# A fused attention and gated feed-forward kernel on one core: value means moved from TensorE to VectorE and DRAM, the sums' check moved up, the order planned anew

## The chip, the cores and the metric

The kernel runs on one core of a Trainium2 chip. The core has four engines that compute (TensorE, VectorE, ScalarE and GpSimd, in the rows PE, DVE, ACT and POOL), a fifth, SyncE (SP), that issues most of the transfers, and 16 DMA engines that carry them out. PE has two rows: PE for matmuls and PEld for the weight loads that go with them. The metric is the time of one execution on the device in microseconds. The kernel before has a median of 662.69 us over three runs (660.53, 662.69 and 663.2).

## The reference

There are four batch elements, eight heads, 768 rows of sequence and 64 columns per head. Attention is a local window of 15 rows to each side joined with 24 summaries of blocks of 32 rows: the key of a summary is the elementwise maximum over its block, its value the mean. The rows of the output, 3072 tokens of 512, then go through a feed-forward of width 2048 whose activation is h - tanh(h).

```python
k_sum = k.reshape(B, H, nb, 32, D).max(axis=3)
v_sum = v.reshape(B, H, nb, 32, D).mean(axis=3)
scores_l = q @ k.T / 8, masked to |i - j| < 16
scores_s = q @ k_sum.T / 8 + log(32)
a = softmax(concat(scores_l, scores_s)); x = a @ concat(v, v_sum)
h = x @ w_in; out = (h - tanh(h)) @ w_out
```

## The kernel before

The sequence is cut into eight units `u` of 384 rows, two for each of the four batch elements `b = u // 2`. A unit has four pairs of heads `p`, and two groups `g` of four heads each. For each pair there is a chain: queries and keys are turned (by TensorE for u = 0 and 1, by VectorE after that), the block maxima are taken (`top max`), scores are formed on TensorE (`scores`), VectorE takes row minima (`min`), ScalarE exponentials (`exp`), the rows are normalized (`normal`), the probabilities turned (`p turn`: TensorE for u = 0 and 1, and VectorE with a trip through DRAM after that), and `values` multiplies them with the tile `vw`, which holds the window's rows of v and, in its first 24 partitions, the 24 means. `x split` writes the result as a high and a low float32r part.

The feed-forward runs 22 slots behind. For each unit there are 16 columns `f` of 128: `in` forms h in the tile pH by 12 matmuls of 384 columns, ScalarE and VectorE or GpSimd make the activation of it, it is split into a high and a low part (`gh`, `gl`), and `out` adds the product with w_out into three tiles pY by 9 matmuls of 512 columns (for u = 0 by three full float32 ones, which the trace shows as two records each). While u = 0 and 1 run, the 32 weight tiles are loaded and converted from float64 by VectorE, ScalarE and GpSimd (`w scale`, `w low`, `w sign`, `w join`, `w high part`, `w low part`).

**The value means.** For b = 0 and 1, `first_means` loads v of a group as one transfer, adds pairs of rows (`pair`, on GpSimd), and `sum_means` adds the rest up with three float32 matmuls against a 0 and 1/32 matrix that lies in the buffer `vacc` (task `sum`); ScalarE copies the result to `mean`. For b = 2 and 3, `sum_chunks` loads a group in four chunks into `tmp`, and VectorE adds eight rows at a time into `vacc` (task `chunk sum`); then `finish_v` turns the sums by four matmuls against the identity (task `mean turn`), and ScalarE scales them by 1/32 into `mean`. `put_mean` carries `mean` into `vw`: two copies for u = 0, one DMA (`mean put`) from then on.

**The sums' check.** The activation is a series that holds for small h. ScalarE collects the sum of h squared of every `in`. At the end VectorE takes the maximum over all of them (`seen`), TensorE turns it (`seen turn`), VectorE takes the maximum again (`seen max`), and every engine loads that number into a register and branches: if it is too large, the whole work is done again in a more general form. The last three copies of pY and their stores stand behind this load in program order, and the branch behind them.

**The order.** Tasks are recorded with their costs and dependencies; `Plan.schedule` then lays them out on five engines by a list schedule, taking the ready task of the highest level. A level is the longest path to the end by the tasks' costs, plus a number per task from the table `BIAS` and one per kind and phase from `KB`. While TensorE would be idle in the first 100 us, the planner puts in matmuls on the identity (`keep_warm`, in the order `pX<-ident`). Each engine then runs its list strictly in order, with semaphores between the lists. All instructions are issued through one helper, which is why every row of the profile has line 65.

Of the kernel before, what the change touches and what calls it, by code (L numbers as in the profile page):

```python
# [10 lines left out]
F32 = mybir.dt.float32  # L11
# [10 lines left out]
SLOTS = 4  # L22
# [295 lines left out]
def program(  # L318
# [211 lines left out]
    def convert(i):  # L530
# [41 lines left out]
        def join():  # L572
            low, _, w = words()
            vector.scalar_tensor_tensor(at(to[0]).bitcast(U32), w.bitcast(U32), 3, low, op0=ALU.logical_shift_left, op1=ALU.bitwise_or)
        either("w scale", {ACT: 0.59, DVE: 0.335, POOL: 1.25}, scale, r=[RAW[1]], w=[(tmp, 0)])
        do("w low", DVE, 0.335, low_bits, w=[RAW[0]])
        either("w sign", {DVE: 0.57, ACT: 1.15}, sign, r=[RAW[1]], w=[RAW[0]])
        do("w join", DVE, 0.66, join, r=[RAW[0], (tmp, 0)], w=[to])
        if not whole:
            either("w high part", {ACT: 0.52, DVE: 0.335, POOL: 1.25}, lambda e: copy(e, at(res)[:, 0], at(tmp)), r=[(tmp, 0)], w=[(res, 0)])  # L580
            either("w low part", {POOL: 1.225, DVE: 0.602}, lambda e: e.tensor_tensor(at(res)[:, 1], at(tmp), at(res)[:, 0].bitcast(F32), op=ALU.subtract), r=[(tmp, 0), (res, 0)], w=[(res, 1)])
# [57 lines left out]
    def first_means(b, g):  # L639
        base = ("V", b, g)  # L640
        buf(base, "vsum1", [P, HG, 6 * D]) if b else buf(base, "xh", [P, HG, 6 * D], F32, 2)
        dma("v load", lambda e: e.dma_start(at(base), v[b, HG * g:HG * (g + 1)].rearrange("h (r t) d -> r h (t d)", t=6)), S * HG * D * 4, 1536, w=[(base, 0)])

        def pairs():
            x = at(base).rearrange("p h (t two d) -> p (h t) two d", two=2, d=D)
            return x[:, :, 0], x[:, :, 1]
        either("pair", {POOL: 1.77, DVE: 0.87}, lambda e: e.tensor_tensor(pairs()[0], *pairs(), op=ALU.add), w=[(base, 0)])

    def sum_means(b, g, tag):
        base, ps = ("V", b, g), bank(("mv", b, g), tag)  # L650
# [7 lines left out]
        do("mean out", ACT, 0.39, lambda: scalar.activation(mean[32 * g:32 * g + NB], at(ps)[:NB, :HG * D], AF.Copy), r=[(ps, 0)], w=[MEAN[g]])  # L658


    def sum_chunks(b, g):
        acc = buf(("acc", b, g), "vacc", [P, 2, D])
        for c in range(4):
# [489 lines left out]
```

## Time and profile before

| | |
|---|---|
| median of three runs | 662.69 us |
| the profiled execution's own time | 662.02 us |
| its span | 660.3 us |
| mean granted TensorE clock | 0.995 |
| PE, PEld busy | 98%, 83% |
| DVE, ACT, POOL busy | 50%, 59%, 28% |
| HBM read, written | 54.39 MB, 15.73 MB |

The rows are of one execution, whose own time is 662.02 us; 1.7 us of it lie outside the span of its instructions. A busy share is an average over a start in which transfers and the small chains of the first unit set the pace, a stretch in which the weights are converted beside the feed-forward of the first unit, and a long even stretch. A matmul record's end is modelled and consecutive records overlap, so what a matmul costs in a dense stretch is the distance from its start to the next start, which the chain of waits shows for runs of records.

### The profile page before, as it was taken

The numbers are of one execution on the slowest core, as the hardware profiler recorded it, in microseconds if no ns is written. First come the engines' busy times: TensorE is split into PE (matmuls) and PEld (weight loads), VectorE is DVE, ScalarE is ACT, GpSimd is POOL, SyncE is SP. The second block draws the span as 40 slices with busy tenths as digits, with TensorE's granted clock in tenths as the row PEclk, the third lists the DMA queues.
The fourth block names the chain that finished last, engine by engine and source line by source line (L and its number), as shares of the span: only waits on it lengthen the run. The fifth ranks groups of instructions, "written<-read, shape, count | busy, mean of one in ns | idle before, by whom it ended". The sixth has DMA issues, their size and how long they took to land.

```text
span 660.3 us, 14416 instructions
## 1 busy us (share of the span) xinstructions
PE 646.4 (98%) x5301; PEld 550.2 (83%) x5301; DVE 331.1 (50%) x1070; ACT 390.1 (59%) x1166; POOL 186.9 (28%) x190
## 2 busy tenths in 40 slices
PE   8999999999999999999999999999999999999995
PEld 6676666688888888889888888898989899899994
DVE  4898898998745675435454543314332433111111
ACT  4898889766546656465555636455654736364442
POOL 3030313134334232233223133322322313122221
PEclk9899999999999999999999999999999999999999
DMA  9978876653665665253453631423303331000001
GB/s 283 242 222 239 221 209 200 100 126 97 143 132 111 158 140 133 62 157 93 84 118 73 171 78 38 93 84 90 78 13 93 108 92 49 1 32 17 1 1 51
DMA packets 157163, 73.18 MB, mean 111 GB/s; under 512 B 120768, under 2 KB 147360, under 8 KB 157088
## 3 DMA queue, kind: packets, MB, share of 16 engines
q1 hardware_dynamic: 156816, 72.01, 43.7%
q8 instruction: 43, 0.70, 0.5%
q14 instruction: 32, 0.26, 0.1%
q10 hardware_dynamic: 272, 0.20, 0.1%
HBM read 54.39 MB, written 15.73 MB: 106 GB/s over the span
## 4 chain that ended last, share of the span: by engine, by line
PE 87%; DMA 5%; DVE 3%; ACT 2%; SPq 1%; issue 1%; POOL 0%; ACTq 0%; DVEq 0%
PE pY L65 39%; PE pH L65 39%; PE pS L65 3%; PE pT L65 3%; PE pX L65 2%; DMA xl<-in_k_dram 2%; DMA raw<-in_moe_w_out_dram 1%; SPq L65 1%; DMA tmp<-in_v_dram 1%; DMA raw<-in_moe_w_in_dram 1%; ACT tmp L65 1%; ACT raw L65 1%; DVE prob L65 1%; DVE tmp L65 0%; DVE raw L65 0%
## 5 line engine op out<-in xcount | busy, mean ns | idle before, releaser
L65 PE MATMUL pH<-xh,w 128*128 128x384 f32 x1024 | 269.6, 344 | 0.4 <-POOL w L65 0.4
L65 PEld LDWEIGHTS pH<-xh,w 128*128 128x128 f32 x1024 | 184.9, 188 | 15.1 <-issue 3.1
L65 POOL TENSOR_TENSOR gl<-gu,gh 128x384 fp32r<-128x384 f32 x112 | 114.2, 1020 | 253.0 <-ACT gh L65 232.7
L65 PE MATMUL pY<-wf,gh 128*128 128x512 f32 x411 | 168.5, 441 | 0.0
L65 DVE TENSOR_TENSOR gu<-gu,gt 128x384 f32<-128x384 f32 x72 | 40.9, 568 | 218.7 <-ACT gu L65 199.8
L65 PE MATMUL pH<-xl,w 128*128 128x384 f32 x448 | 150.6, 336 | 0.0
L65 ACT ACTIVATE gu<-pH 128x384 f32<-128x384 f32 x128 | 62.6, 489 | 146.5 <-PE pH L65 138.4
L65 ACT ACTIVATE gh<-gu 128x384 fp32r<-128x384 f32 x109 | 57.2, 525 | 72.6 <-DVE gu L65 40.1
L65 PEld LDWEIGHTS pY<-wf,gh 128*128 128x128 f32 x411 | 76.6, 188 | 24.9 <-issue 14.1
L65 ACT ACTIVATE prob<-prob,stats 128x118 f32<-128x118 f32 x207 | 78.2, 385 | 14.2 <-DVE stats L65 14.1
L65 PEld LDWEIGHTS pH<-xl,w 128*128 128x128 f32 x448 | 84.0, 188 | 0.0
L65 POOL TENSOR_TENSOR gu<-gu,gt 128x384 f32<-128x384 f32 x40 | 41.3, 1031 | 119.0 <-ACT gu L65 113.6
L65 ACT ACTIVATE gu<-gu 128x384 f32<-128x384 f32 x128 | 67.0, 523 | 0.0
L65 ACT ACTIVATE gt<-pH 128x384 f32<-128x384 f32 x128 | 62.0, 484 | 0.8 <-PE pH L65 0.8
L65 PE MATMUL pY<-kT,gh 128*128 128x512 f32 x126 | 50.4, 400 | 0.0
L65 PE MATMUL pY<-kT,gl 128*128 128x512 f32 x126 | 49.6, 394 | 0.3 <-POOL gl L65 0.3
L65 DVE TENSOR_SCALAR prob<-prob,stats 128x118 f32<-128x118 f32 x177 | 49.3, 344 | 0.8
L65 PE MATMUL pY<-vsum,gh 128*128 128x512 f32 x105 | 41.8, 398 | 0.0
L65 PE MATMUL pY<-vsum,gl 128*128 128x512 f32 x105 | 40.9, 390 | 0.0
L65 ACT ACTIVATION_READ_ACCUMULATOR prob<-prob,stats 128x1 f32 x192 | 36.5, 190 | 0.0
L65 DVE CUSTOM_DVE_ANT_0 prob<-pS,mask 128x118 f32<-128x118 f32 x96 | 25.4, 277 | 17.5 <-PE pT L65 16.2
L65 DVE TENSOR_SCALAR raw<-raw 128x512 uint32<-128x512 uint32 (+1 forms) x51 | 28.4, 570 | 2.2 <-DMA raw<-in_moe_w_out_dram 1.0
(155 smaller groups left out, 961.3 us busy)
## 6 DMA issues: line engine op xcount, KB each, us to landing
place<-turned SPq DMA_DIRECT2D x96, 96.0 KB, 1.9
probT<-place SPq DMA_DIRECT2D x24, 384.0 KB, 3.5
raw<-in_moe_w_in_dram SPq DMA_DIRECT2D x16, 512.0 KB, 4.0
raw<-in_moe_w_out_dram SPq DMA_DIRECT2D x16, 512.0 KB, 4.5
vw<-in_v_dram SPq DMA_DIRECT2D x80, 96.0 KB, 4.2
out_dram<-tmp SPq DMA_DIRECT2D x23, 256.0 KB, 2.1
rawq<-in_q_dram SPq DMA_DIRECT2D x96, 48.0 KB, 2.1
raw<-in_k_dram SPq DMA_DIRECT2D x48, 96.0 KB, 2.9
```

The source lines that it names most:

```text
L65: return lambda *args, **kwargs: self._tc.keep_in_program_order(op(*args, **kwargs))
```

## The change

For b = 1 to 3, all value means now come from `sum_chunks`: VectorE adds eight rows of a chunk into the second half of `vacc`, and a second instruction scales by 1/32 and adds to the first half (or, for the first chunk, only scales). The sums leave `vacc` by a DMA to DRAM (`mean save`, 96 rows of 256 bytes, written in the order of blocks), and `mean put` reads them from there for u = 2 to 7. `finish_v` is gone, and `first_means` and `sum_means` are called for b = 0 alone. The chunks of b = 1 are recorded while u = 1 is scored.

The three tasks of the check are recorded ahead of the last `out` (function `look`), and the `out` tasks of the second and third tile wait until `seen turn` has been issued. The last copies and stores still follow the load.

The planner's costs of a dozen kinds are changed, and `BIAS`, `SL` and `KB` are new tables.

```diff
-BIAS = {('const', 0): -83.15, ('const', 1): 88.23, ('const', 2): -15.03, ...
+BIAS = {('const', 0): 151, ('const', 1): 13.25, ('const', 2): 155, ...
...
-        either("w sign", {DVE: 0.57, ACT: 1.15}, sign, r=[RAW[1]], w=[RAW[0]])
-        do("w join", DVE, 0.66, join, r=[RAW[0], (tmp, 0)], w=[to])
+        either("w sign", {DVE: 0.54, ACT: 1.1}, sign, r=[RAW[1]], w=[RAW[0]])
+        do("w join", DVE, 0.61, join, r=[RAW[0], (tmp, 0)], w=[to])
...
-        buf(base, "vsum1", [P, HG, 6 * D]) if b else buf(base, "xh", [P, HG, 6 * D], F32, 2)
+        buf(base, "xh", [P, HG, 6 * D], F32, 2)
...
     def sum_chunks(b, g):
         acc = buf(("acc", b, g), "vacc", [P, 2, D])
...
-                vector.tensor_reduce(m[:, 1 if c else 0], x.rearrange("r t d -> r d t"), axis=AX.X, op=ALU.add)
+                vector.tensor_reduce(m[:, 1], x.rearrange("r t d -> r d t"), axis=AX.X, op=ALU.add)
                 if c:
-                    vector.tensor_tensor(m[:, 0], m[:, 0], m[:, 1], op=ALU.add)
-            do("chunk sum", DVE, 1.22 if c else 0.97, total, w=[(st, 0), (acc, 0)])
-
-    def finish_v(b, g):
-        acc, ps = ("acc", b, g), bank(("mv", b, g), "pT")
-
-        def go():
-            for hh in range(HG):
-                tensor.matmul(at(ps)[:NB, D * hh:D * (hh + 1)], ident[:96, NB * hh:NB * (hh + 1)], at(acc)[:96, 0], start=True, stop=True)
-        do("mean turn", PE, 0.557, go, r=[(acc, 0), IDENT], w=[(ps, 0)])
-        do("mean out", ACT, 0.39, lambda: scalar.activation(mean[32 * g:32 * g + NB], at(ps)[:NB, :HG * D], AF.Copy, scale=1.0 / 32), r=[(ps, 0)], w=[MEAN[g]])
+                    vector.scalar_tensor_tensor(m[:, 0], m[:, 1], 1.0 / 32, m[:, 0], op0=ALU.mult, op1=ALU.add)
+                else:
+                    vector.tensor_scalar(m[:, 0], m[:, 1], 1.0 / 32, None, op0=ALU.mult)
+            do("chunk sum", DVE, 1.25 if c else 1.1, total, w=[(st, 0), (acc, 0)])
+        place = buf(("means", b, g), "means", [NB, HG, D], F32, 2 * NG, scratch)
+        dma("mean save", lambda e: e.dma_start(at(place).rearrange("n h d -> h n d"), at(acc)[:96, 0]), 96 * 256, 256, r=[(acc, 0)], w=[(place, 0)])
...
+        if u >= WHOLE:
+            place = ("means", u // 2, g)
+            dma("mean put", lambda e: e.dma_start(at(vw)[:NB].rearrange("r i f h d -> r (i f) (h d)"), at(place).rearrange("n h d -> n (h d)").unsqueeze(1).broadcast_to([NB, 2 * NT, HG * D])), 2 * NT * NB * HG * D * 4, 1024, r=[(place, 0)], w=[vw_keys(vw, i, half)[2] for i in range(NT) for half in range(2)])
+            return
...
-            do("out", PE, 0.86 if whole else 0.702, go, r=keys, w=[(y, 0)])
+            do("out", PE, 0.86 if whole else 0.702, go, r=keys, w=[(y, 0)], before=[t for t in plan.tasks if t.kind == "seen turn" and i])
...
+    def look():
+        st, ps = share(("st", "seen"), "stats", 2, lambda n: made[("stats",)][:, n]), bank(("seen",), "pT")
+        do("seen", DVE, 0.2, lambda: vector.tensor_reduce(at(st)[:, 0:1], sums_seen, axis=AX.X, op=ALU.max), r=[(SEEN, n) for n in range(NM)], w=[(st, 0)])
+        do("seen turn", PE, 0.1, lambda: tensor.transpose(at(ps)[:1, :P], at(st)[:, 0:1], ident), r=[(st, 0), IDENT], w=[(ps, 0)])
+        do("seen max", DVE, 0.2, lambda: vector.tensor_reduce(seen, at(ps)[:1, :P], axis=AX.X, op=ALU.max), r=[(ps, 0)])
...
+            if small_only and m2 == (NU - 1, NF - 1):
+                look()
             moe_out(*m2)
...
-        if B > 1 and j in (20, 28):
-            first_means(1, (j - 20) // 8)
-            sum_means(1, (j - 20) // 8, "pT")
-        if s0 is not None and not early and s0[0] % 2 == 1 and 1 < s0[0] < NU - 1:
+        if s0 is not None and not early and s0[0] % 2 == 1 and s0[0] < NU - 1:
             b, (n, c) = s0[0] // 2 + 1, divmod(j % (NP * SLOTS), SLOTS)
             if n % 2 == 0 and c == 0:
                 sum_chunks(b, n // 2)
-            elif n % 2 == 1 and c == SLOTS - 1:
-                finish_v(b, n // 2)
-
-    if small_only:
-
-        st, ps = share(("st", "seen"), "stats", 2, lambda n: made[("stats",)][:, n]), bank(("seen",), "pT")
...
```

At the start, SP's queue, before: `xl<-in_k_dram` is the keys of one pair of heads of u = 0 (the row with x2 is those of the second and third pair), `xh<-in_v_dram` a whole group of v for the means of b = 0, `vw` the window's rows of v, `raw` a weight tile.

```order
L65 DMA rawq_108<-in_q_dram 128x2x192
L65 DMA xl<-in_k_dram 128x2x384
L65 DMA vw_128<-in_v_dram 16x4x64
L65 DMA rawq_96<-in_q_dram 128x2x192
L65 DMA xl<-in_k_dram 128x2x384 x2
L65 DMA xh<-in_v_dram 128x4x384 x2
L65 DMA raw<-in_moe_w_in_dram 128x4x256
L65 DMA xl<-in_k_dram 128x2x384
L65 DMA vw_98<-in_v_dram 16x4x64
L65 DMA vw_98<-in_v_dram 96x4x64 x2
```

All four pairs' keys stand ahead of the window's rows of v, the last behind one weight tile. The same stretch of SP's queue now, from the keys of the second pair on (those of the first pair and 192 KB of queries stand ahead of it):

```order
L65 DMA xl<-in_k_dram 128x2x384
L65 DMA rawq_130<-in_q_dram 128x2x192
L65 DMA xh<-in_v_dram 128x4x384 x2
L65 DMA raw<-in_moe_w_in_dram 128x4x256 x2
L65 DMA raw<-in_moe_w_out_dram 128x1024
L65 DMA vw_98<-in_v_dram 16x4x64
L65 DMA vw_98<-in_v_dram 96x4x64 x3
L65 DMA xl<-in_k_dram 128x2x384
L65 DMA vw_98<-in_v_dram 96x4x64
L65 DMA rawq_130<-in_q_dram 128x2x192
L65 DMA rawq_96<-in_q_dram 128x3x64
L65 DMA xl<-in_k_dram 128x2x384
```

Three weight tiles and four pieces of `vw` have moved ahead of the keys of the third pair, and more queries ahead of those of the fourth.

On VectorE, before, the place of the first chunk sums (those of b = 2): `vacc<-tmp` adds the eight rows of a chunk, `vacc<-vacc` adds them to the rest, `prob` is a normalization, ISA the row minima.

```order
L65 RECIPROCAL stats<-stats 128x6
L65 STREAM_TRANSPOSE rawq_96<-rawq_96 128x384
L65 TENSOR_REDUCE vacc<-tmp 96x64
L65 TENSOR_SCALAR prob<-prob,stats 128x118
L65 MEMSET pS 64x15
L65 ISA prob,stats<-pS,mask 128x118
L65 ISA stats 128x1
L65 TENSOR_REDUCE vacc<-tmp 96x64
L65 TENSOR_TENSOR vacc<-vacc 96x64
L65 TENSOR_SCALAR prob<-prob,stats 128x118 x5
L65 ISA prob,stats<-pT,mask 128x118
```

On VectorE now, the place of the first chunk sums (those of b = 1), among the conversion of weights (`raw`, `qa`, `wl`) and the activation of u = 0 (`gh<-gu,gt`):

```order
L65 TENSOR_SCALAR raw<-raw 128x512
L65 TENSOR_REDUCE vacc<-tmp 96x64
L65 TENSOR_SCALAR vacc<-vacc 96x64
L65 COPY probT<-pT 118x384
L65 TENSOR_REDUCE vacc<-tmp 96x64
L65 SCALAR_TENSOR_TENSOR vacc<-vacc 96x64
L65 TENSOR_TENSOR gh<-gu,gt 128x384
L65 SCALAR_TENSOR_TENSOR qa<-qa,raw 128x512
L65 TENSOR_TENSOR xl<-pX,xh 128x384
L65 TENSOR_TENSOR wl<-wf_450,kT 128x512
```

The chunk sums now begin earlier in the program, beside the conversion of the last weight tiles, and eight more of them stand on VectorE; the second instruction is a scale or a scale and add.

On TensorE, the end of the program before: `pY` are the three output tiles, `pT<-ident,stats` is `seen turn`.

```order
L65 MATMUL pY_7034<-vsum_1676,gl 128x512
L65 MATMUL pY_7028<-vsum_1676,gh 128x512
L65 MATMUL pY_7028<-wf_2270,gh 128x512
L65 MATMUL pY_7028<-vsum_1676,gl 128x512
L65 MATMUL pT<-ident,stats 1x128
L310 TENSOR_LOAD seen
L313 COMPARE_AND_BRANCH
```

On TensorE now, the place of `seen turn`, near the end:

```order
L65 MATMUL pY_7053<-vsum_1392,gh 128x512
L65 MATMUL pY_7053<-wf_2108,gh 128x512
L65 MATMUL pY_7053<-vsum_1392,gl 128x512
L65 MATMUL pT<-ident,stats 1x128
L65 MATMUL pY_7025<-vsum_1392,gh 128x512
L65 MATMUL pY_7025<-wf_2141,gh 128x512
L65 MATMUL pY_7025<-vsum_1392,gl 128x512
```

`seen turn` has moved from behind the last `out` to a place with 27 matmuls of `out` behind it, the last of which is followed by the load and the branch.

## Rows read from the trace of the kernel before

**Rows 1.** The page: the span, and each engine's busy time and share.

```profile
span 660.3 us, 14416 instructions
...
PE 646.4 (98%) x5301; PEld 550.2 (83%) x5301; DVE 331.1 (50%) x1070; ACT 390.1 (59%) x1166; POOL 186.9 (28%) x190
```

**Rows 2.** Windows: length, busy time of each engine, clock, DMA share, GB/s.

```profile
20.00:44.00 24.00, 21.12 (x318) 15.79 (x317) 20.30 (x77) 20.52 (x61) 4.42 (x3) 0.93 0.87 242
44.00:165.00 121.00, 120.75 (x922) 87.49 (x923) 107.60 (x286) 94.77 (x254) 32.58 (x28) 1.00 0.68 173
165.00:652.00 487.00, 486.67 (x3817) 432.38 (x3816) 191.96 (x658) 262.11 (x811) 142.13 (x139) 1.00 0.35 83
```

**Rows 3.** All waits of PE from 45 to 652 us: total, times, longest.

```profile
PE pY L65 <- POOL gl L65: 0.3, 1, 0.3
PE pH L65 <- POOL w L65: 0.2, 1, 0.2
```

**Rows 4.** Chain of waits, 380 to 392 us: start, duration, what.

```profile
380.73 4.24 PE pH L65 x24
384.97 2.09 PE pY L65 x9
387.06 0.56 PE pT L65 x8
387.62 2.29 PE pH L65 x12
```

**Rows 5.** Instructions by form: count, busy, mean ns, idle before.

```profile
L65 PEld LDWEIGHTS pH<-xh,w 128*128 128x128 f32 x1024 | 184.9, 188 | 15.1 <-issue 3.1 <-POOL w L65 2.2 <-ACT prob L65 0.4
...
L65 PE MATMUL pT<-vsum,vacc 128*24 128x256 f32 x12 | 3.0, 382 | 0.0
...
L65 PE MATMUL pT<-vacc,ident 96*24 96x64 f32 x32 | 2.5, 221 | 0.0
```

**Rows 6.** Chain of waits, 52 to 56 us.

```profile
53.26 1.41 PE pT L65 x6
54.66 1.06 PE pY L65 x2
```

**Rows 7.** Timeline of the tail from 651.8 us: start, duration, instruction, idle before.

```profile
651.87 0.39 PE L65 MATMUL pY<-vsum,gl 128*128 128x512 f32 x1
...
652.10 0.27 PE L65 MATMUL pT<-ident,stats 128*1 128x128 f32 x1
652.41 0.28 DVE L65 TENSOR_REDUCE seen<-pT 1x1 f32<-1x128 f32 x1 [4.16 <-PE pT L65]
653.27 0.60 ACT L65 ACTIVATE qa<-pY 128x512 f32<-128x512 f32 x1 [4.40 <-DVE seen L65]
653.77 1.08 ACT L65 ACTIVATE tmp<-pY 128x512 f32<-128x512 f32 x2
654.38 1.62 SPq L65 DMA_DIRECT2D out_dram<-tmp  x2
```

**Rows 8.** Chain of waits at the start, 0 to 60 us.

```profile
5.85 11.47 DMA xl<-in_k_dram
...
43.49 0.48 DVE vsum L65
```

**Rows 9.** Timeline of DVE, 145 to 147 us, one chunk sum.

```profile
145.24 1.07 DVE L65 TENSOR_REDUCE vacc<-tmp 96x64 f32<-96x512 f32 x1
146.34 0.22 DVE L65 TENSOR_TENSOR vacc<-vacc 96x64 f32<-96x64 f32 x1
146.48 0.66 DVE L65 TENSOR_SCALAR prob<-prob,stats 128x118 f32<-128x118 f32 x3
```

**Rows 10.** Instructions by form: DVE's activation product, of one shape, in two tiles.

```profile
L65 DVE TENSOR_TENSOR gu<-gu,gt 128x384 f32<-128x384 f32 x72 | 40.9, 568 | 218.7 <-ACT gu L65 199.8 <-ACT gt L65 19.0
...
L65 DVE TENSOR_TENSOR gh<-gu,gt 128x384 f32<-128x384 f32 x16 | 12.0, 747 | 3.8 <-PE pY L65 3.6
```

**Rows 11.** DMA issues: count, KB each, median us to landing.

```profile
out_dram<-tmp SPq DMA_DIRECT2D x23, 256.0 KB, 2.1
```

More of the change, by code (lines that the diff above doesn't have):

```diff
@@ new lines @@
+KB = {('chunk load', 0): -847, ('chunk load', 2): 1437, ('chunk sum', 0): 496, ('chunk sum', 2): -1857, ('const', 0): -1655, ('exp', 0): -228, ('exp', 1): 370, ('exp', 2): -4255, ('g', 0): -1202, ('g', 1): 169, ('g', 2): 433, ('g high', 1): -1906, ('g high', 2): -3954, ('g low', 1): -7875, ('g low', 2): 522, ('in', 0): -703, ('in', 1): -535, ('in', 2): -1361, ('in part', 2): -565, ('inverse', 0): -998, ('inverse', 1): -640, ('inverse', 2): 1118, ('k load', 0): -720, ('k load', 1): -1860, ('k load', 2): -3283, ('k out', 0): -227, ('k turn', 0): 1039, ('k turn', 2): -753, ('mean copy', 0): -530, ('mean out', 0): -1876, ('mean put', 1): 1803, ('mean put', 2): 556, ('mean save', 2): -4261, ('min', 0): -195, ('min', 1): -2343, ('min', 2): -515, ('normal', 0): 756, ('normal', 1): -1338, ('normal', 2): -299, ('out', 0): 2635, ('out', 1): -1226, ('out', 2): 233, ('p load', 0): 448, ('p load', 1): -5773, ('p load', 2): 1937, ('p out', 0): -67.7, ('p out', 1): -3011, ('p save', 0): 204, ('p save', 1): -9402, ('p save', 2): 543, ('p turn', 0): -387, ('p turn', 1): 573, ('p turn', 2): -167, ('pair', 2): 3803, ('q load', 0): -172, ('q load', 1): 2452, ('q load', 2): 421, ('q out', 0): 1860, ('q out', 1): 883, ('q turn', 0): 1683, ('q turn', 1): 26.28, ('q turn', 2): -4070, ('scores', 0): 406, ('scores', 1): 774, ('scores', 2): -251, ('seen', 2): 5132, ('seen max', 2): -6233, ('seen turn', 2): 3598, ('series', 0): -4082, ('series', 1): 305, ('series', 2): -4266, ('square', 0): -859, ('square', 1): 179, ('square', 2): -2313, ('sum', 0): 131, ('sum guard', 0): -19.21, ('sum guard', 1): 1520, ('sum guard', 2): 382, ('tanh', 0): 212, ('tanh', 1): 209, ('tanh', 2): -2500, ('top max', 0): 380, ('top max', 2): -4604, ('v load', 0): -429, ('v load', 1): -1772, ('v load', 2): 1045, ('values', 0): -13.56, ('values', 1): -190, ('values', 2): 347, ('w high part', 0): -7630, ('w high part', 1): 1043, ('w high part 2', 0): -4978, ('w high part 2', 1): -2608, ('w high part 2', 2): -2943, ('w join', 0): -199, ('w join', 1): -2721, ('w join', 2): -1287, ('w load', 0): -100, ('w load', 1): 665, ('w low', 0): -4933, ('w low', 1): -773, ('w low part', 0): -2075, ('w low part', 1): -1362, ('w low part 2', 1): -1780, ('w low part 2', 2): -613, ('w scale', 0): -50.88, ('w scale', 1): -466, ('w sign', 0): 1797, ('w sign', 1): -847, ('w sign', 2): -2233, ('x high', 0): 621, ('x high', 1): -3991, ('x high', 2): 1034, ('x low', 0): 207, ('x low', 1): -241, ('x low', 2): 627, ('y out', 2): -202, ('y store', 2): 1334}
@@ L657, in sum_means @@
         do("sum", PE, 1.405, go, r=[(base, 0), BLK], w=[(ps, 0)])
-        do("mean out", ACT, 0.39, lambda: scalar.activation(mean[32 * g:32 * g + NB], at(ps)[:NB, :HG * D], AF.Copy), r=[(ps, 0)], w=[MEAN[g]])
+        do("mean out", ACT, 0.37, lambda: scalar.activation(mean[32 * g:32 * g + NB], at(ps)[:NB, :HG * D], AF.Copy), r=[(ps, 0)], w=[MEAN[g]])
     def sum_chunks(b, g):
@@ L888, in go @@
                             tensor.matmul(at(px_base(u, x))[64 * a:64 * a + 64, c:c + 64], at(vw)[:N2, n, half, 2 * (x % PG) + a, :], turned_of(u, x, n, a, half), start=True, stop=True)
[L889 removed]
+        do("values", PE, 0.15 + 0.7 * len(pairs), go, r=[(("pt", u, x), n) for x in pairs for n in range(2)] + [key for n in range(NT) for half in range(2) for key in vw_keys(vw, n, half) if key in plan.writer], w=[(px_base(u, x), n) for x in pairs for n in range(NT)])
     def x_split(u, p):
@@ L1098, in program @@
                 sum_chunks(b, n // 2)
-            elif n % 2 == 1 and c == SLOTS - 1:
-                finish_v(b, n // 2)
-    if small_only:
-        st, ps = share(("st", "seen"), "stats", 2, lambda n: made[("stats",)][:, n]), bank(("seen",), "pT")
-        do("seen", DVE, 0.2, lambda: vector.tensor_reduce(at(st)[:, 0:1], sums_seen, axis=AX.X, op=ALU.max), r=[(SEEN, n) for n in range(NM)], w=[(st, 0)])
-        do("seen turn", PE, 0.1, lambda: tensor.transpose(at(ps)[:1, :P], at(st)[:, 0:1], ident), r=[(st, 0), IDENT], w=[(ps, 0)])
-        do("seen max", DVE, 0.2, lambda: vector.tensor_reduce(seen, at(ps)[:1, :P], axis=AX.X, op=ALU.max), r=[(ps, 0)])
     last_stores = set([t for t in plan.tasks if t.kind in ("y out", "y store")][-6:])
```

18 lines of the change are left out of this document (8 added, 10 removed).

## The prediction, made before the changed kernel ran

> **What bounds the kernel.** I read the page first, then windows over the whole span, the waits of PE, the chain of waits in two short windows, the instructions by form, and the timeline of the tail. The page gives PE 98% of a span of 660.3 us [rows 1], and the windows show where the rest is: PE is busy 486.67 of 487.00 us from 165 us on and 120.75 of 121.00 us from 44 to 165 us, at a granted clock of 1.00 (2.4 GHz), and only 21.12 of 24.00 us from 20 to 44 us [rows 2], part of that on identity matmuls that do no work. All that PE waits for between 45 and 652 us comes to 0.5 us [rows 3]. So the program is three pieces: a start up to about 44 us that VectorE and transfers pace (the first unit's last low part ends at 43.49 + 0.48 = 43.97 us, and the feed-forward can run in full from there [rows 8]), 608 us in which PE works without a gap, and a tail of 8 us behind the last `out`. Whatever leaves PE in the middle comes off the time one for one, as long as nothing else falls behind PE.
>
> A busy matmul row alone does not prove that, since records overlap. The chain does: two `in` tasks, 24 matmuls, take 4.24 us, 0.177 us each [rows 4], and one weight load of that kind takes 0.188 us [rows 5]: there PE is held by its own weight loads, back to back. [...]
>
> **PE work removed.** The two `sum` tasks of b = 1 are six records each, 1.41 us from first to the next task's turn [rows 6]; the 12 records are the ones into pT [rows 5]: 2 x 1.41 = 2.8 us. The four `mean turn` tasks are eight records each, 32 in all [rows 5], 0.56 us a task [rows 4]: 4 x 0.56 = 2.2 us. A small task between feed-forward runs also costs the run behind it: the `in` after a `mean turn` took 2.29 us where one of two in a row took 2.12 [rows 4], 0.17 us. By the new order, TensorE's list has 51 such insertions after the start, `seen turn` among them, where it had 53 without that one: 2 x 0.17 = 0.3 us less. `seen turn` itself, 0.27 us [rows 7], used to stand behind the last `out` and now delays it: 0.3 us more. Sum for the middle: -2.8 - 2.2 - 0.3 + 0.3 = -5.0 us. The copies of the means by ScalarE and GpSimd's two additions of pairs go as well; neither engine is waited for by PE for more than 0.3 us at once [rows 3], and I count nothing for them.
>
> **The tail.** Before, the last `out` ends at 651.87 + 0.39 = 652.26 us; then come the transpose of the check, VectorE's maximum at 652.41, the register loads, ScalarE's first copy of an output tile at 653.27, and the third ends at 653.77 + 1.08 = 654.85 us [rows 7]. That is 2.59 us from the last matmul to the last copy, because all three copies stand behind the load. In the new order 27 matmuls of `out` stand between `seen turn` and the end, 27 x 0.23 = 6.2 us at the spacing of nine in 2.09 us [rows 4]. The check needs only VectorE's 0.28 us and a load that before took from 652.69 to 653.27 [rows 7], so it is over when the last tile is done, and two of the three copies can run before. What stays is a hand-over of about 0.1 us and one copy of 0.60 us: 0.7 instead of 2.59, a gain of 1.9 us. Does PE wait at `seen turn`? It needs the square of the last `in` (384 columns on ScalarE, at most the 0.60 us of a copy of 512 [rows 7]) and VectorE's maximum (0.28 us), with three hand-overs of about 0.1: 1.2 us; nine matmuls of `out`, 2.09 us, stand between and cover it. Without that cover it would cost up to 1.2 us. The stores then go out one by one instead of three within a microsecond; one takes 2.1 us to land [rows 11]. If their transfer, and not the last copy, sets the end, the gain is smaller, down to nothing; if it had queued before, larger. I take 1.9.
>
> **VectorE.** Eight chunk sums are added. One takes 1.24 us, from the reduction's start at 145.24 to the next instruction's at 146.48 [rows 9]; the new second instruction reads the same 64 columns and I give it the same time: 8 x 1.24 = 9.9 us, nearly all in the stretch before 165 us, and a scale of 0.14 us for each of four older first chunks, which fall where VectorE is busy 191.96 of 487 us [rows 2] and cost nothing. In 44 to 165 us VectorE is busy 107.60 of 121 us [rows 2]. 117.5 us would hardly fit. But its records there are stretched: the product of the activation takes 747 ns in the tile that only u = 0 uses and 568 ns later, for the same shape [rows 10]; and PE waits for almost nothing there [rows 3], so the list has slack. Bounds: 0, and 9.9 us if every microsecond ends at PE. I take 1.0, nearer to the row that says PE waited 0.5 us in all; the idle that absorbed the lateness of conversions gets short. The Trainium skill, VectorE: DVE Perf Modes, section Rules for kernel authors, calls the reduction the slowest operation of this engine and advises to restructure it away from a hot path. By the 0.96 GHz on that page 512 columns are 0.53 us, an estimate, and eight of them would cost 4.3 us instead of the 8.6 that eight reductions of 1.07 us come to; the trace decides, and the advice is the reason for the slower rival.
>
> **The trip through DRAM.** `mean save` and `mean put` stand on SP's queue with other transfers between, and `mean put` waits for the save to land, with chunk loads of later groups queued behind. A transfer of ten times its size lands in 2.1 us [rows 11]. In the new order the first such `mean put` stands some seven columns of `in` and `out` (4.2 us each [rows 4]) ahead of the `values` that needs it: nothing.
>
> **The start.** Nothing in its work changes, but its order does. The last keys landed at 5.85 + 11.47 = 17.3 us [rows 8], with 4.2 MB in front of them by the queue's order, all in all some 0.28 MB a microsecond from about 2 us on. Now the third pair's keys have 5.2 MB up to them and the fourth's 6.0 MB, which makes 20.7 and 23.5 us, an estimate from that rate. Before, the third pair's turn started right when the keys were there; 3.1 us later is the upper bound if that chain sets the end of the start. On the other side, VectorE was idle 24.00 - 20.30 = 3.7 us from 20 to 44 us [rows 2], and weight tiles now come earlier, which gives it work in the gaps: at best 3.7 us earlier. Four more identity matmuls stand in the list. I take 0.
>
> **Sum**, against the profiled execution: 662.0 - 5.0 - 1.9 + 1.0 + 0 = 656.1 us. That execution lies 0.7 us under the median of 662.69; I keep 656.1 for the median too. What a measurement can tell from no change is about 0.5%, 3.3 us: faster is below 659.4, slower above 666.0.
>
> **Rivals.**
> - The start gets shorter by VectorE's 3.7 us: 652.4 us. For it: the gaps. Against: the last pair's keys arrive 6 us later.
> - The stores set the end, and the tail gains nothing: 658.0 us. For it: three stores of 256 KB were under way together before. Against: the span's end lies 5.4 us behind the last copy, more than a store takes.
> [...]
> - Half of the chunk sums' 9.9 us reaches PE, 5.0 instead of 1.0: 660.1 us. For it: 89% busy. Against: stretched records.
> - Slower: VectorE becomes the bound of 44 to 165 us. If it can't get above the share that it had, 107.6 of 121 us, then 117.5 us of work take 132.1 us; that is 11.1 us more, and the `sum` tasks removed there gain nothing. With `mean turn` (2.2) and the tail (1.9) still gained: 662.0 + 11.1 - 4.1 = 669.0 us. It decides from the point at which the stretch gets 4.1 us longer than before, that is if VectorE stays under 117.5 of 125.1 us, 94%. For it: in-order lists, and the conversion of weights beside it. Against: before, the same engine kept PE fed although it had 13.4 us to spare.
>
> **Chances.** Forecast 0.57, shorter start 0.11, tail without gain 0.08, together 0.76 faster; room on PE 0.06 and half of the chunk sums 0.11, together 0.17 within 0.5%; VectorE as the bound 0.07, slower. The range for 8 in 10 goes from the short start, 652.0, to a little over the two cases at 660.1, 661.5; the forecast's own range, with the start off by 2 us either way and VectorE between 0 and 2.5, is 653.5 to 658.5.
>
> **What would show it.** In the new profile: PE busy in every window from about 44 us to the end of the last `out`, at clock 1.00, with that end about 5 to 4 us earlier; no rows pT<-vsum,vacc and pT<-vacc,ident; PE's waits between 45 us and the end under 2 us; the last copy of pY less than 1 us behind the last matmul; 24 reductions into `vacc`, the first eight before 165 us; the last `x low` of u = 0 at 42 to 46 us. The forecast is wrong if PE waits for DVE or for a weight tile by several microseconds between 100 and 170 us, or if the full feed-forward starts later than 47 us.

## The result, and the profile after

The changed kernel takes 651.25 us (median of four runs, 650.83 to 651.82) where the kernel before takes 662.25 us beside it: ratio 0.9837, interval 0.9815 to 0.9860. The kernel got faster, as forecast, but by more: 656.1 us was said, and 651.25 lies 0.75 us under the range. Beside runs 1 to 4 below, one of the 13 runs of the kernel before took 1266.75 us, for a reason that nothing here shows; the ratios leave it out.

The head of the page after, the answer to [rows 1]:

```profile
span 649.1 us, 14381 instructions
...
PE 638.0 (98%) x5265; PEld 547.6 (84%) x5265; DVE 344.1 (53%) x1091; ACT 391.7 (60%) x1167; POOL 175.7 (27%) x180
```

PE is busy 8.4 us less than before, VectorE 13.0 us more. The windows after, with the columns of [rows 2]:

```profile
20.00:44.00 24.00, 21.08 (x392) 17.30 (x392) 20.99 (x83) 20.56 (x59) 3.99 (x3) 1.00 0.86 216
44.00:165.00 121.00, 120.90 (x883) 89.45 (x883) 113.07 (x298) 94.41 (x258) 31.49 (x27) 1.00 0.67 175
165.00:640.00 475.00, 475.00 (x3747) 423.64 (x3746) 199.21 (x657) 263.71 (x812) 132.79 (x130) 1.00 0.35 85
```

VectorE now fills 113.07 of 121 us from 44 to 165 us, 93%, and PE still runs without a gap; from 45 to 640 us no wait of PE is listed at all, where [rows 3] has two (the view lists no wait under 0.15 us). One chunk sum after (timeline of VectorE; start, duration, instruction), to be read beside [rows 9]. Element two is b = 1; its eight sums run from 114.9 to 138 us, where the kernel before has its first chunk sum, of element three, at 143.1 us:

```profile
116.63 1.07 DVE L65 TENSOR_REDUCE vacc<-tmp 96x64 f32<-96x512 f32 x1
...
117.74 0.22 DVE L65 SCALAR_TENSOR_TENSOR vacc<-vacc 96x64 f32<-96x64 f32 x1
117.88 0.55 DVE L65 TENSOR_TENSOR gh<-gu,gt 128x384 f32<-128x384 f32 x1
```

It takes 1.25 us from its start to the next instruction's start; the price of 1.24 us was right. The tail after, beside [rows 7]:

```profile
642.72 0.60 ACT L65 ACTIVATE qa<-pY 128x512 f32<-128x512 f32 x1 [2.42 <-PE pY L65]
...
643.34 0.34 SPq L65 DMA_DIRECT2D out_dram<-qa  x1
643.40 1.28 ACT L65 ACTIVATE tmp<-pY 128x512 f32<-128x512 f32 x2
...
643.65 0.39 PE L65 MATMUL pY<-vsum,gl 128*128 128x512 f32 x1
644.02 1.43 SPq L65 DMA_DIRECT2D out_dram<-tmp  x2
```

The last `out` ends at 643.65 + 0.39 = 644.04 us, the last copy at 643.40 + 1.28 = 644.68, 0.64 us behind it instead of 2.59. From the last `out` to the end of the span it is 5.1 us instead of 8.0.

The feed-forward runs in full from here on:

```profile
46.50 1.88 PE L65 MATMUL pY<-wf,gh 128*128 128x512 f32 x4
```

So the two profiles part in three places: the first full `out` starts at 46.50 instead of 48.10 us (-1.6), from there to the end of the last `out` it is 597.5 instead of 604.2 us (-6.6), and the tail is 3.0 us shorter. Forecast were 0, -4.0 and -1.9.

### The profile page after: what moved, and what is told of

It reads as the page before. It is cut to its first block, busy times and chain, and to the rows that moved or that the text cites. A ratio compares the mean times of both kernels' runs of the same rounds, so it can differ in the third digit from the quotient of the medians.

```text
span 649.1 us, 14381 instructions
## 1 busy us (share of the span) xinstructions
PE 638.0 (98%) x5265; PEld 547.6 (84%) x5265; DVE 344.1 (53%) x1091; ACT 391.7 (60%) x1167; POOL 175.7 (27%) x180
## 4 chain that ended last, share of the span: by engine, by line
PE 85%; DVE 7%; ACT 4%; DMA 3%; issue 1%; DVEq 0%; ACTq 0%
PE pY L65 39%; PE pH L65 39%; PE pS L65 3%; PE pT L65 3%; DVE raw L65 2%; PE pX L65 2%; DVE prob L65 2%; DMA raw<-in_moe_w_in_dram 2%; ACT prob L65 1%; ACT raw L65 1%; DMA raw<-in_moe_w_out_dram 1%; DMA rawq<-in_q_dram 1%; DVE wf L65 1%; DVE top L65 1%; ACT tmp L65 0%
## 5 line engine op out<-in xcount | busy, mean ns | idle before, releaser
L65 DVE TENSOR_TENSOR gu<-gu,gt 128x384 f32<-128x384 f32 x77 | 49.1, 638 | 193.9 <-ACT gu L65 193.7
L65 ACT ACTIVATE prob<-prob,stats 128x118 f32<-128x118 f32 x201 | 76.7, 386 | 23.9 <-DVE stats L65 23.7
L65 POOL TENSOR_TENSOR gu<-gu,gt 128x384 f32<-128x384 f32 x35 | 37.0, 1057 | 100.8 <-ACT gu L65 89.8
L65 DVE TENSOR_SCALAR prob<-prob,stats 128x118 f32<-128x118 f32 x183 | 52.1, 349 | 0.7
L65 DVE TENSOR_SCALAR raw<-raw 128x512 uint32<-128x512 uint32 (+1 forms) x54 | 31.3, 587 | 3.2 <-DMA raw<-in_moe_w_in_dram 1.8
```

The costliest lines, as they stand in the source:

```text
L65: return lambda *args, **kwargs: self._tc.keep_in_program_order(op(*args, **kwargs))
```

## The experiments

Sixteen runs followed, one of them (run 12) of the kernel before as it is; the expectations below count them by these numbers. Where no ratio stands, the difference is one of medians, across sets of runs. The median of the kernel before was 661.2 to 662.5 us in the six sets, so such a difference can be off by about 1 us.

**The check (runs 1, 2 and 5).** Run 1 is the kernel before with the check moved up alone:

```diff
-            do("out", ..., r=keys, w=[(y, 0)])
+            do("out", ..., r=keys, w=[(y, 0)], before=[t for t in plan.tasks if t.kind == "seen turn" and i])
...
+            if small_only and m2 == (NU - 1, NF - 1):
+                look()
             moe_out(*m2)
...
```

> The kernel before with one edit: the check of the sums stands ahead of the last two output tiles, everything else in its old order. Theory (the tails of the two traces, 8.04 us from the end of the last out before and 5.06 after): the tail alone gets 3.0 us shorter, the transpose costs TensorE about 0.1 us in its new place, so 662.25 - 2.9 = 659.4 us. Rival (the prediction's sum: only the two copies that no longer stand behind the load, 1.9 us, and 0.3 us for the transpose): 660.65 us. Rival (the short tail after comes from the new order, not from the check): 662.0 to 662.5 us.

Measured: 658.48 us, ratio 0.9964 (0.9951 to 0.9977), 2.4 us (1.5 to 3.2) less. With the order kept, the tail is 5.7 us instead of 8.0: the check alone makes most of the short tail.

Run 2 takes both edits out of the changed kernel and records the check at the end.

> The changed kernel with the check put back behind the last output tile, everything else in the new order. Theory: the same 2.9 us the other way, 651.25 + 2.9 = 654.15 us, with a tail of 8.0 us. Rival of 1.6 us: 652.85 us. Rival (the order made the tail): 651.3 us.

Measured: 652.40 us, but it is no test: the planner still laid the transpose nine matmuls of `out` ahead of the end, and the last copy still ends 0.63 us behind the last `out`. Its 1.15 us came from elsewhere (last section). Run 5 has the edits of run 2 and forces the transpose to the end:

```diff
-        do("seen turn", PE, 0.1, ..., w=[(ps, 0)])
+        do("seen turn", PE, 0.1, ..., w=[(ps, 0)], before=[t for t in plan.tasks if t.kind == "out"][-NT:])
```

> The changed kernel with the check's transpose forced behind the last matmul of out, as before (in the second run the planner had put it only ten matmuls further back, with three copies that hardly waited). Order otherwise unchanged. Theory (the check's place is worth what the first run showed, 2.4 us, to the 3.0 us between the tails): 653.7 to 654.3 us, tail about 8 us. Rival (only the 1.15 us of the second run): 652.4 us.

Measured: 653.78 us, 2.5 us over the changed kernel. Its timeline shows the old sequence again, with the copies behind the maximum:

```profile
643.95 0.27 PE L65 MATMUL pT<-ident,stats 128*1 128x128 f32 x1
644.25 0.28 DVE L65 TENSOR_REDUCE seen<-pT 1x1 f32<-1x128 f32 x1 [4.18 <-PE pT L65]
645.12 0.60 ACT L65 ACTIVATE qa<-pY 128x512 f32<-128x512 f32 x1 [4.09 <-DVE seen L65]
```

The check's place is worth about 2.5 us in either order.

**TensorE's work (run 6).**

```diff
+                if WHOLE <= u < 7 and f in (2, 5, 8, 11, 14) or u == 7 and f in (2, 5, 8):
...
+                    tensor.matmul(at(ph)[:, :U], high[:, 0], at(xh)[:, 0], start=True, stop=True)
                 go(range(NC))
```

> The changed kernel with 28 matmuls of in done once more (five of the sixteen in tasks of the units from element two on, three in the last unit; the task's own first matmul overwrites them), order unchanged: 28 x 0.177 = 5.0 us of TensorE behind 165 us. Theory (work there comes one for one): 651.25 + 5.0 = 656.2 us. Rival (matmuls lie in room that weight loads leave): 651.3 to 652 us.

Measured: 656.31 us, 5.06 us for 28 matmuls counted at 0.177, or 0.181 each. The added work costs its time one for one; behind 165 us TensorE has no room for it.

**VectorE (runs 4, 13, 7, 14, 9).** Run 4 doubles the eight first reductions, run 13 every second one of them (`b == 1 and c % 2`), run 14 the sixteen later ones (`b > 1`):

```diff
-                vector.tensor_reduce(m[:, 1], ...)
+                for _ in range(2 if b == 1 else 1):
+                    vector.tensor_reduce(m[:, 1], ...)
```

> The changed kernel, each of the eight first reductions of chunks done twice with the same result, order unchanged: eight more instructions of about 1.07 us, 8.6 us of VectorE in 105 to 135 us. Theory A (VectorE's records are stretched and it has slack although it is busy 113.07 of 121 us in 44 to 165 us): at most 1.5 us more, 651.3 to 652.8 us. Rival B (93% is its limit; 121.7 us don't fit into 121): 4 to 8.6 us more, 655 to 660 us, with waits of TensorE for VectorE or for what it hands on.

> The changed kernel with every second one of the eight first reductions done twice (4 x 1.07 = 4.3 us of VectorE more in 105 to 135 us), order unchanged. With all eight twice (8.6 us) TensorE waited 6.0 us and lost 3.4 us more at half the granted clock behind the longest wait. Theory A (VectorE has 8.6 - 6.0 = 2.6 us to give, then every microsecond is a wait): 1.7 us of waits, no wait long enough for the clock to fall, 653.0 us; with a stretch of 3.41 us at half the clock 654.7 us. Theory B (it has nothing to give): 4.3 us, 655.5 us, or more with the clock. Theory C (the price starts only beyond 4.3 us): 651.3 us.

> The changed kernel with the sixteen later reductions (elements three and four) done twice: 16 x 1.07 = 17 us of VectorE more, nearly all behind 200 us, where VectorE is busy 199 of 475 us. Order unchanged. Theory (the price of a sum hangs on its place: behind 200 us it lies beside other work): 651.3 to 652 us, although twice as much is added as in the fourth run. Rival (a reduction holds up the list wherever it stands, as in-order lists do): 655 us or more.

Measured: 659.62 us with eight (8.6 us of VectorE, 8.4 us of time), 652.94 us with four (4.3 us, 1.7 us), 657.02 us with the sixteen (17 us, 5.8 us). The waits of PE in run 4, 44 to 645 us (PE's tile and line, what it waited for: us in all, times, longest):

```profile
PE pY L65 <- ACT tmp L65: 3.7, 1, 3.7
PE pY L65 <- DVE gh L65: 1.7, 1, 1.7
PE pH L65 <- POOL w L65: 0.6, 1, 0.6
```

They are 6.0 us, and the window behind the longest has a granted clock of 0.77:

```profile
135.00:150.00 15.00, 11.29 (x90) 10.13 (x89) 14.12 (x21) 5.20 (x13) 3.37 (x4) 0.77 0.26 84
```

A mean of 0.77 over 15 us is 6.9 us at 1.2 GHz, half of which is lost: 3.5 us. 6.0 + 3.5 = 9.5, and the stretch from the first full `out` to the last is 9.4 us longer than in the changed kernel. The chain of waits shows what the longest hangs on: VectorE's sums up to 142.4 us, then the copy of an output tile into the buffer that they held, then PE (start, duration, what):

```profile
140.37 0.98 DVE vacc L65
141.37 1.02 DVE vacc L65
142.41 0.61 ACT tmp L65
...
143.06 1.22 PE pY L65 x2
```

In run 13 PE waits 1.9 us in all, none over 0.7:

```profile
PE pY L65 <- DVE gh L65: 1.2, 2, 0.7
PE pH L65 <- POOL w L65: 0.4, 1, 0.4
PE pS L65 <- PE pH L65: 0.3, 1, 0.3
```

Theory A of run 13 (VectorE has 2.6 us to give, then each microsecond is a wait) fits its 1.7 us; but 1.7 us is little more than sets of runs differ by, so the 2.6 is an estimate from two runs. Nor do all of these waits come from the doubled sums: run 6, which adds nothing to VectorE, has a wait of 0.9 us for `gh` and one of 0.4 us for `w` at 92 to 96 us, ahead of the sums. The wait of 3.7 us in run 4 is the one that cost clock. Theory A of run 4, at most 1.5 us for eight, was wrong. Run 14 was expected to cost nothing and did not; its rival, 655 us or more, holds. Behind 165 us VectorE is busy 45% in it, and PE has five kinds of waits, 3.5 us in all, the longest 1.0 us; the first three:

```profile
PE pH L65 <- ACT gt L65: 1.0, 1, 1.0
PE pT L65 <- DVE xl L65: 0.8, 1, 0.8
PE pY L65 <- POOL gl L65: 0.7, 2, 0.4
```

Nothing of the kind is listed there in the changed kernel. The other 2.3 us of the 5.8 are in no listed wait.

Run 7 leaves seven of the first eight sums out:

```diff
             def total(c=c, st=st):
+                if b == 1:
+                    if c == 0:
+                        vector.tensor_scalar(at(acc)[:96, 0], at(st)[:96, :D], 1.0 / 32, None, op0=ALU.mult)
+                    return
```

> The changed kernel without the sums over the chunks of element two (its block means are not computed; the loads of the chunks and the hand-overs stay): 7 of 8 reductions and their second instructions, some 9 us of VectorE before 140 us, are left out, order unchanged. Theory (the new order hides the eight sums fully, TensorE waits 0 us behind them): 651.0 to 651.5 us. Rival A (they cost the forecast's 1.0 us): 650.2 us. Rival B (what one more costs, one less gives back, one for one as in the fourth run): 642 to 645 us.

Measured: 651.70 us, ratio 0.9853 (0.9821 to 0.9885): no gain. VectorE falls to 102.98 of 121 us from 44 to 165, and the stretch from the first full `out` to the last takes 597.9 us, where the changed kernel has 597.5. The new order hides the eight sums, as far as runs that spread over 2.7 us can tell.

Run 9 is run 4 with buffers of their own for element two's chunks:

```diff
-            st = buf(("ch", b, g, c), "tmp", [P, 8 * D], F32, 2)
+            st = buf(("ch", b, g, c), "ck" if b == 1 else "tmp", [P, 8 * D], F32, 2)
```

> The fourth run (the eight first reductions twice) with one more edit: the chunks of element two land in two buffers of their own and no longer in the two of tmp, which the conversions of weights had before them and the output tiles of the first unit have behind them. Order unchanged. In the fourth run TensorE waited 3.7 us for a copy of an output tile into tmp, 1.7 us for VectorE's gh, 0.6 us for a weight, and then ran 6.83 us at half the granted clock (3.4 us lost): 9.4 us in all. Theory (the shared buffers hand VectorE's lateness to TensorE): the 3.7 us and the 3.4 us behind them go, 659.6 - 7.1 = 652.5 us. Rival (VectorE is simply full, and the next thing that it owes is late instead): 657 to 660 us.

Measured: 660.62 us, just above the rival's 657 to 660. The wait for `tmp` is gone, and the waits of PE still sum to 6.0 us:

```profile
PE pS L67 <- issue: 2.8, 1, 2.8
PE pY L67 <- DVE gh L67: 2.4, 2, 1.8
PE pH L67 <- POOL w L67: 0.8, 2, 0.4
```

The shared buffers were where the lateness came out, not its cause. For the longest of these waits (`issue`) the profile shows nothing that the engine waited for.

**The order (runs 3, 10, 8, 11).** Run 3 has the changed kernel's operations in the old order. The list of before is written out, and tasks are taken by their rank in it as their dependencies allow:

```diff
+        for n, (e, kind, i) in enumerate(x.split(":") for x in ORDER.split()):
...
+        while todo:
+            t = heapq.heappop(todo)[2]
+            done.append(t)
```

> The changed kernel's operations (new means, no sums and turns on TensorE for elements two to four, check ahead) in the order of the kernel before: each engine's list is that of before without what is gone, and the new instructions stand at the TensorE task where the changed kernel has them. Theory A (work decides, the added VectorE time is covered in either order): 5.0 us of TensorE work and 0.3 us of insertions and 2.9 us of tail come off, the start and the other waits stay as before: 662.25 - 8.2 = 654.0 us, and the full feed-forward starts at 48.1 us as before. Rival B (the chunk sums don't fit between the conversions of weights unless the order is planned around them): TensorE waits between 105 and 170 us for several microseconds, 656 to 660 us. Rival C (the order is worth nothing): 651.3 us.

Measured: 671.96 us, ratio 1.0168 (1.0155 to 1.0182): slower than either kernel, and worse than rival B. What VectorE waited for longest from 44 to 165 us, and, in the second block, what PE waited for longest:

```profile
DVE vacc L67 <- DMA tmp<-in_v_dram: 10.3, 4, 4.5
```

```profile
PE pY L67 <- DVE gh L67: 4.8, 1, 4.8
PE pS L67 <- DVE stats L67: 3.5, 1, 3.5
```

VectorE stood at chunk sums for loads that waited for `tmp`, with the `gh` and the statistics that PE needs queued behind. Run 10 adds the edit of run 9 to it.

> The third run (the changed kernel's operations in the order of before) with the chunks of element two in two buffers of their own. In the third run VectorE stood 10.3 us at chunk sums for loads, four times, with the gh and the weights that TensorE needs queued behind. Theory (the old order fails because loads that wait for tmp block VectorE's list, not because VectorE has no time): the loads come early, 672 - 10 to 14 = 658 to 662 us. Rival (VectorE has too much to do in that stretch in the old order): 668 us or more.

Measured: 666.05 us, ratio 1.0077 (1.0063 to 1.0091): between theory and rival. VectorE's wait for chunk loads falls to 1.0 us, the time by 6 us; the rest of the loss has other causes in that order, which no run takes apart. Run 8 is the mirror image: the old means (with the check ahead) in the new order.

> The means as before (element two by GpSimd and TensorE, the turns of the sums of elements three and four on TensorE), the check ahead, every engine's list that of the changed kernel, with the old instructions at the TensorE task where the kernel before has them. Theory (the work is worth its 5.3 us on TensorE, and the new order is neutral for the rest): 651.25 + 5.3 = 656.5 us. Rival A (the order is the gain, not the means): 651 to 653 us. Rival B (the order of before is as good for the old means as the new one, and this mixture disturbs): 658.5 us, as the first run, or more.

Measured: 666.29 us, ratio 1.0070 (1.0043 to 1.0098). That is rival B (658.5 us or more): the mixture disturbs, by 10 us over the 656.5 us that the work gives. In both mixtures the foreign instructions were merged in by a simple rule, so they show what an unplanned order can cost, not what a planned one would, and they do not tell what the new order by itself is worth. Run 11 gives the changed kernel the buffers of run 9.

> The changed kernel with the chunks of element two in two buffers of their own, order unchanged. TensorE waits for nothing behind 51 us in it, so both theories say no change: 651.0 to 651.5 us. If it gets slower, the earlier loads take bandwidth from weights; if faster by over 1 us, the trace hides a wait.

Measured: 650.58 us, ratio 0.9849 (0.9834 to 0.9864), against 0.9837 (0.9815 to 0.9860) of the changed kernel: the same.

**The start and the waits of the kernel before (runs 12, 15, 16).**

> The kernel before once more, unchanged, for its start: in its first profile TensorE's granted clock is 0.5 for 3.41 us from 25.9 us on, and the first full out starts at 48.1 us; in the other profiles with the same list of the start (first and third run) there is no such stretch and it starts at 46.2 and 45.8 us. Theory (that stretch comes and goes from execution to execution, and costs half of its length): without it 46.2 to 46.5 us and a span of 658.4 to 658.8 us, with it 48.1 us and 660.3 us. Rival (the start of the kernel before is slower by its order): 48 us without any such stretch.

Measured: 46.34 us for the first full `out`, but a span of 660.9 us: half of the theory. Windows of 20 to 30 us (PE, PEld, DVE, ACT, POOL, clock, DMA share, GB/s), the first full `out` and one later matmul, of the first profile of the kernel before:

```profile
20.00:30.00 10.00, 8.39 (x121) 5.69 (x122) 7.76 (x36) 7.42 (x26) 0.00 (x0) 0.83 0.99 270
```

```profile
48.10 1.45 PE L65 MATMUL pY<-wf,gh 128*128 128x512 f32 x3
...
122.11 1.12 PE L65 MATMUL pH<-xh,w 128*128 128x384 f32 x2
123.08 0.34 PE L65 MATMUL pH<-vsum,w 128*128 128x384 f32 x1
```

and of run 12, the same program:

```profile
20.00:30.00 10.00, 8.64 (x161) 6.60 (x159) 8.61 (x39) 9.18 (x31) 0.00 (x0) 1.00 1.04 272
...
44.00:125.00 81.00, 79.41 (x537) 52.90 (x530) 70.64 (x183) 68.44 (x168) 19.55 (x15) 1.00 0.71 197
```

```profile
46.34 1.88 PE L65 MATMUL pY<-wf,gh 128*128 128x512 f32 x4
...
110.08 0.44 PE L65 MATMUL pH<-xh,w 128*128 128x384 f32 x1 [1.05 <-DVE w L65]
...
122.99 0.44 PE L65 MATMUL pH<-xh,w 128*128 128x384 f32 x1 [0.15 <-POOL w L65]
123.27 0.34 PE L65 MATMUL pH<-vsum,w 128*128 128x384 f32 x1
```

In run 12 the full feed-forward starts 1.76 us earlier, PE then waits for weight tiles at 109, 117 and 122 us, and the same matmul stands at 123.27 instead of 123.08 us. By these two profiles alone something other than PE would pace the kernel before up to there. But run 1, whose list of PE is the same up to the tail, starts as early and keeps its lead:

```profile
46.21 1.88 PE L65 MATMUL pY<-wf,gh 128*128 128x512 f32 x4
...
121.12 0.44 PE L65 MATMUL pH<-xh,w 128*128 128x384 f32 x1 [0.15 <-POOL w L65]
121.40 0.34 PE L65 MATMUL pH<-vsum,w 128*128 128x384 f32 x1
```

So there is no fixed pace: one execution starts 1.8 us late, behind a stretch of lower clock, one waits 1.6 us for weight tiles, and one does neither. The changed order has small waits for weights too, 0.3 to 0.4 us in runs 2, 5, 6 and 7. Two runs were meant to name the resource. Run 15 takes 5.9 us of VectorE out of the kernel before, run 16 most of the bytes of two loads of v:

```diff
-                    either("normal", ..., lambda e, i=i, a=a: normal(e, i, a), ...)
+                    either("normal", ..., lambda e, i=i, a=a: None if u == 1 else normal(e, i, a), ...)
```

> The kernel before without the 24 scalings of the probabilities of the second unit (its rows are not divided by their sums; the threshold of the check is raised so that it takes the same path); order unchanged. 18 of them, 5.9 us of VectorE, lie between 56 and 100 us, ahead of the conversions of weights that TensorE waited for at 108.6 to 123 us in the second profile of the kernel before. Theory (the conversions set the time up to 123 us, whatever TensorE could do: the same task starts at 122.80 and 122.99 us in two profiles whose starts differ by 1.76 us): the waits there go, about 2 us, 661.3 - 2 = 659.3 us, and the task at 123 us starts at 120.5 to 121.5 us. Rival (TensorE's own work sets that time): 661.3 us, less what is in the noise.

```diff
+        hs = 1 if b else HG
-        dma("v load", lambda e: e.dma_start(at(base), v[b, HG * g:HG * (g + 1)]...
+        dma("v load", lambda e: e.dma_start(at(base)[:, :hs], v[b, HG * g:HG * g + hs]...
...
```

> The kernel before, with one head of four in each of the two loads of v that its means of element two need at 32 and 59 us (192 instead of 768 KB; the other three heads' means are copies of the first's); order unchanged. The changed kernel has these loads as chunks behind 108 us. 1.15 MB less among the loads of weights is 5.5 us of transfers at the 210 GB/s of 20 to 125 us. Theory (the transfers set when weights are converted, and these set TensorE's time up to 123 us): the waits up to there go, 661.3 - 2 = 659.3 us, and the task that started at 122.80 and 122.99 us starts by 121 us. Rival (weights wait for VectorE and ScalarE, not for transfers): 661.3 us, the task at 122.8 to 123 us.

Measured: 661.67 us, ratio 0.9991 (0.9974 to 1.0008), and 661.54 us, ratio 0.9990 (0.9975 to 1.0005): no difference that can be told. Their first full `out` starts at 46.37 and 46.17 us, PE's waits up to 125 us are 0.3 and 0.9 us, and the matmul stands at 121.91 and 122.58 us, between those of run 1, which has neither edit, and run 12. So neither edit can be given the credit, and what makes the weights late in one execution and not in another stays open.

## Why the prediction missed

The signs that the prediction named came: PE without a gap at clock 1.00, both kinds of row gone, the last copy 0.64 us behind the last matmul, eight sums before 165 us. One did not: the last `out` was to end 4 to 5 us earlier and ends 8.2 us earlier. What leaves TensorE and the tail did come off the time, as said; but three terms of the sum were mis-sized, all to the same side.

**TensorE's work, -2.8 and -2.2 us: right as a price.** Run 6 gives 5.06 us for 5.0 of such work. The Trainium skill, Perfetto Trace Analysis, section Identifying the Most-Contended Engine, says to judge TensorE's headroom by MFU (the share of its peak arithmetic) and by the busy share of weight loads, not by matmul busy time. Read by the weight loads alone, 83% would leave room, and run 6 would have ended near 651 us; the measured 656.31 us shows none ("room on PE", chance 0.06).

**The tail, "I take 1.9", and "0.3 us more" for the transpose: mis-sized.** Net 1.6 was said, 2.5 measured (run 5). The copies gained what was said, 2.59 - 0.64 = 1.95. On top, the end of the span lies 4.4 us behind the last copy instead of 5.4; over all runs it is 4.2 to 5.0 us with the check ahead and 5.4 to 6.1 with the check last, but also 6.0 in run 2, whose copies did not wait. The prediction named this case ("if it had queued before, larger") and took nothing for it; what the 1.0 us hangs on is not shown. 1.95 + 1.0 - 2.5 leaves some 0.4 for the transpose, near the 0.3 said.

**"VectorE. ... I take 1.0": mis-sized, nothing in the end.** Run 7 shows no cost, so the sum carried 1.0 too much. Its reason, that "the list has slack" because PE waited for little, does not hold as it stands: in the new order four more reductions cost 1.7 us and eight 8.4 (runs 13 and 4), and in the old order the same operations make the kernel slower (run 3). The slower rival, 669.0 us with a chance of 0.07, is near what run 3 measured, 671.96, though by another way: VectorE was not full there (99.07 of 121 us from 44 to 165 us), it stood at loads. The Trainium skill, VectorE: DVE Perf Modes, section Rules for kernel authors, advises to consider restructuring reductions that lie on a hot path; here they cost nothing where the order was planned with them, and 5.8 us for 17 in run 14 where it was not. One reduction is 1.07 us in the trace.

**The order, taken as neutral: the step that failed.** "Nothing in its work changes, but its order does. ... I take 0" priced the start at nothing, and in the middle the small waits were counted at nothing and the insertions at 0.3 us. Run 1 and the changed kernel both have the check ahead and the same start (46.21 and 46.50 us), and differ by the means and the order: 658.48 against 651.25 us, 7.2 us, of which the work taken off TensorE is 5.0. From the first full `out` to the end of the last it is 604.8 against 597.5 us. The other 2.2 us are the new order or what else left with the old means; no run takes these two apart.

Part of it can be seen in the pair of profiles that the prediction compared, where the middle is 6.6 us shorter and 5.0 of that is the work. The longest wait of [rows 3], listed as 0.3 us, holds up two matmuls of the kernel before:

```profile
378.12 0.39 PE L65 MATMUL pY<-wf,gh 128*128 128x512 f32 x1
378.84 0.50 PE L65 MATMUL pY<-kT,gl 128*128 128x512 f32 x1 [0.33 <-POOL gl L65]
379.18 0.40 PE L65 MATMUL pY<-kT,gh 128*128 128x512 f32 x1
```

From 378.12 to 379.18 us are 1.06 us for two matmuls that take 0.46 at the usual 0.23: 0.6 us, gone after. The remaining 1.0 us is in small pieces, among them the feed-forward runs that the `mean turn` tasks used to cut.

The start is another matter. Its 1.6 us come from one execution: in the first profile of the kernel before the granted clock is 0.83 from 20 to 30 us, and the four others with that list (runs 1, 12, 15 and 16) start at 46.2 to 46.4 us, as early as the changed kernel. For the order the "0" of the start was nearly right; against the one execution from which the sum was taken it was not. That execution's own time is near the median all the same; run 12, at 662.67 us, lost time to waits for weights instead. The changed kernel's four runs lie within 1.0 us of each other.

How the conversion of weights moved can be seen in VectorE's windows on the tiles `raw` (weights and keys) of the kernel before, and then of the changed kernel (length, busy time, clock, DMA share, GB/s):

```profile
80.00:105.00 25.00, 12.11 (x22) 1.00 0.72 199
105.00:135.00 30.00, 14.25 (x20) 1.00 0.70 148
```

```profile
80.00:105.00 25.00, 18.56 (x27) 1.00 0.78 231
105.00:135.00 30.00, 9.22 (x13) 1.00 0.66 147
```

6.5 us more of that work is done between 80 and 105 us, and the eight sums follow from 114.9 us on, partly in the 5.0 us that it takes less from 105 to 135 us. The rival of a shorter start, 652.4 us, came nearest to the time by luck: it has 3.7 us from VectorE's gaps ahead of 44 us, and the start gave 1.6 for another reason.

**The sum.** In the two profiles it closes: 1.6 for the start, 5.0 for the work, 1.6 for the rest of the middle and 3.0 for the tail are 11.2 us, and the spans differ by 660.3 - 649.1 = 11.2. By medians the check gives 2.5 and the step from run 1 to the changed kernel 7.2, together 9.7 of 11.0 us (interval 9.3 to 12.3 by the ratio); the other 1.3 is no more than the medians of the kernel before differ by from set to set.

## What to carry to other kernels

One profile is one execution. Before a stretch is called bound by an engine, or late by its order, take more profiles of the same list and compare the time of one and the same instruction: here it stood at 123.08, 123.27 and 121.40 us in three of them, and two would have misled. Price an edit together with the order that comes with it; the same operations were worth 11 us less in a planned order and 10 us more in a kept one. And ask of added work how much fits until the first wait: here nothing was paid for the eight sums, 1.7 us for 4.3 us more and 8.4 us for 8.6 us more, 3.5 of it in the clock behind one long wait.

## What the runs showed of the hardware that was not expected

**Issuing the last two stores takes SyncE 0.9 to 2.6 us.** In run 2 the three stores of the tail go out as

```profile
643.25 0.34 SPq L65 DMA_DIRECT2D out_dram<-qa  x1
643.78 2.55 SPq L65 DMA_DIRECT2D out_dram<-tmp  x2
```

The last two take 2.55 us there, where they take 1.43 us in the changed kernel and 1.62 us in [rows 7]; they take 2.63 us in run 5 and 0.91 us in run 16. The 1.12 us over the changed kernel are about the 1.15 us by which run 2 is slower. What makes an issue long was not tested.

**TensorE's clock after a wait.** It went to the lower level, 1.2 GHz, behind the wait of 3.7 us in run 4 and not behind the waits of up to 0.7 us in run 13. And one and the same program had a granted clock of 0.83 between 20 and 30 us in one profile and 1.00 in another.
